# Soft-MoE behind biased attention on one core: last tokens in other buffers, output layers as ordered steps, a new order

## Chip, cores and metric

The kernel runs on one core of one Trainium2 chip. The metric is device microseconds (us) for one execution; the kernel before takes 542.05 us (median of 3 runs, 541.92 to 543.41).

## What is computed

All numbers are float32. First an attention with 8 batches, 8 heads, 576 tokens and 64 numbers a head, with a bias from a small network of the distance between tokens:

```python
scores = scale * np.matmul(q, k.transpose(0, 1, 3, 2))
x = (psi_rel / psi_i)[..., None]
h = np.maximum(x @ w1 + b1, 0.0)
bias = h @ w2
scores = scores + bias.transpose(2, 0, 1)[None, :, :, :]
attn = exp(scores - max) / (sum + 1e-09)
return np.matmul(attn, v)
```

Then a soft mixture of experts over the 4608 tokens of 512 numbers, with 8 experts of 4 slots and hidden size 1024:

```python
logits = x @ phi
slot_input = softmax(logits, axis=0).T @ x
h = np.maximum(slot_input[e] @ w1[e], 0.0)
slot_out[e] = h @ w2[e]
return softmax(logits, axis=1) @ slot_out
```

The softmax over tokens (axis 0) runs over all batches, so the expert layers can begin only when the last batch has been through the attention.

## The kernel before

**Units.** The work is cut into 32 units, one for a pair of heads (hp = 0 to 3) and a batch (b = 0 to 7); unit u is hp * 8 + b. A unit has five (even u) or four blocks p of 128 query rows. A block goes through two score steps S{p}.0 and S{p}.1 on TensorE (PE; 320 and 256 key columns, both heads in each; with a "+" as four 64x64 tiles, line 431, else as two tiles of 64x128, line 425), four steps t{p}.{head}{pass} on VectorE (DVE, line 451) that take the scores out of PSUM, add the bias and keep the running minimum (pass 1 of a head starts from the minimum of pass 0), two exponents e on ScalarE (ACT, line 462), sums m on DVE (469, 470), two scalings n on GpSimd (POOL, 357), transposes T and R on PE (406), copies c and cR out of PSUM (360), and then the product with the values M0, M1, Mr (549), copied out by x0 and x1 to tile xts. The units of hp 0 to 2 write xts to the tensor xs in HBM.

**Tokens.** The units 24 to 31 (hp = 3) fetch the other three head pairs of their batch back from xs: step fx, line 575, tile xo of one buffer, 864 KB. From it come the transposed tokens (K01, K23, KR, copies kc, krc), the logits (L, line 624, copy lc), their repetition over the slots (D), maxima and exponents (d1, d2, d3), the turned weights (W, wc; C, then cA, cB, cC for the softmax over slots) and the sum over tokens (Z, zc). Unit 30 also joins the state of the first seven batches (J1 to J8, F1 to F3).

**Expert layers.** turn_slots() turns the collected slots (line 981); first(j), j = 0 to 7, makes 16 products of 512 columns each (line 996, float32 products show as two instructions); hidden(Q) and turn_hidden(Q) apply the ReLU and turn the result; second(k, Q) is the second layer (1044), gather_slots(k) repeats the slots (1055), and put(k, q) and put_rest(k) multiply by the softmax over slots (1074), copy the products out of PSUM (1024 numbers a row for each half z: z = 0 on ACT, 1 on DVE) and write them out (1083, 1090). The stacked slot weights cT and cR come from the steps A0, A1 with copies Ac0, Ac1 (lines 1024, 1027, 1032, 1033).

**Weights.** 64 tiles of 512 KB, in the order in which the layers need them (fetch_w, lines 874 to 882). 23 go to the buffers "w" during the attention, 24 to buffers that the attention gives back at the end (steps wbm, wbr, wy, wqk, wat, wv, wxo, wxt, wxk), and 17 are refetched to "w" buffers that the first layer has read.

**Order.** Every step is listed by name and unit in ORDER; the program issues the steps sorted by that list, and each engine runs its instructions in that order. All DMAs are issued by SyncE (SP), in the same order, so a DMA that waits for a buffer holds back those behind it. What follows the list was plain code:

```python
for _, _, f in sorted(prog, key=lambda x: x[:2]):
    f()
turn_slots()
for j in range(4):
    first(j)
    refetch(*range(4 * j, 4 * j + (4 if j < 3 else 2)))
hidden(0)
```

Of the kernel before, what the change touches and what calls it, by code (L numbers as in the profile page):

```python
# [36 lines left out]
f28.2/-1 f27.3/-1+ f27.2/-1 f27.1/-1 f34.3/-1 D22/-1 E19/-1 f30.2/-1 B29/-1 E29/-1 f30.0/-1+ D18/-1 D16/-1 f30.1/-1 f34.1/-1
B28/-1 E28/-1 B27/-1 E27/-1 f30.3/-1 f34.2/-1+ D23/-1 D21/-1 D17/-1 f34.0/-1 f24.3/-1+ S1.0/0+ t1.00/0 t1.10/0 f31.2/-1 B30/-1
E30/-1 f31.1/-1 f31.0/-1 f31.3/-1 f24.0/-1+ B34/-1 f24.2/-1 f35.3/-1 E34/-1 f24.1/-1+ f35.0/-1 D19/-1 S0.0/0+ B31/-1 f32.2/-1
f32.1/-1 f35.1/-1 D29/-1 f35.2/-1 B24/-1 f32.0/-1+ f32.3/-1+ D33/-1 E31/-1 t0.10/0 D28/-1 D27/-1 B32/-1 E32/-1+ E24/-1 B35/-1  # L40
S0.1/0 S1.1/0+ E35/-1 S2.0/0 D30/-1 t0.00/0 t0.01/0 t0.11/0 e0.0/0 t1.11/0 e1.1/0 e0.1/0 b2/-1 t1.01/0 e1.0/0 t2.10/0 S2.1/0+
t2.11/0 S3.0/0 D34/-1 e2.1/0 t2.00/0 m0/0 t2.01/0 S0.0/1 D31/-1 D24/-1 D32/-1 n0.1/0 S0.1/1+ e2.0/0 t0.00/1 D35/-1 t0.10/1 t0.01/1
e0.0/1 n0.0/0 S3.1/0 t0.11/1 m1/0 e0.1/1 m2/0 b3/-1 t3.00/0 t3.01/0 t3.10/0 T0/0 c0/0 S4.0/0 n1.1/0 n1.0/0 m0/1 R1/0 n2.1/0 n0.0/1
e3.0/0 t3.11/0 e3.1/0 T1/0 cR1/0+ S4.1/0 S1.0/1 n0.1/1 b4/-1 t4.00/0 t4.10/0 c1/0 S2.0/1 t4.01/0 m3/0 e4.0/0 t4.11/0 t1.10/1
e4.1/0 n2.0/0 t1.00/1 n3.1/0 T2/0 t2.10/1 c2/0 m4/0 S1.1/1 t1.11/1 t2.00/1 n3.0/0 T3/0 t1.01/1 S2.1/1 T0/1 n4.1/0 n4.0/0 c3/0
t2.11/1 t2.01/1 R3/0 cR3/0+ T4/0 w1/8 e1.0/1 R4/0 cR4/0+ c4/0 e2.1/1 S3.0/1+ t3.00/1 t3.10/1 e2.0/1 m2/1 S3.1/1+ e1.1/1 t3.11/1
e3.1/1 m1/1 n2.1/1 lq/2 t3.01/1 e3.0/1 n1.0/1 M0/0 lq/3 M1/0 Mr/0 c0/1 n2.0/1 m3/1 x1/0 x0/0+ S0.0/2+ t0.00/2 t0.10/2 n1.1/1 T1/1
R1/1 cR1/1+ n3.0/1 c1/1 S0.1/2 t0.11/2 t0.01/2 T2/1 c2/1 S1.0/2 n3.1/1 R3/1 cR3/1 t1.10/2 T3/1 c3/1 e0.1/2 t1.00/2 S1.1/2+ t1.01/2
t1.11/2 S3.0/2+ t3.00/2 t3.10/2 lv/2 S2.0/2+ t2.10/2 e0.0/2 m0/2 n0.1/2 t2.00/2 S3.1/2+ t3.01/2 e1.0/2 t3.11/2 e1.1/2 w0/8 M0/1
S2.1/2+ S4.0/2 M1/1 m1/2 e3.0/2 t2.11/2 n0.0/2 t2.01/2 t4.10/2 e3.1/2 m3/2 e2.1/2 e2.0/2 t4.00/2 S4.1/2 t4.11/2 e4.1/2 m2/2 n1.1/2  # L50
n1.0/2 Mr/1 t4.01/2 x0/1 n3.0/2 n3.1/2 T3/2 e4.0/2 lv/3 x1/1+ R1/2 cR1/2 c3/2+ T0/2 c0/2 m4/2 S1.0/3 n2.1/2 t1.10/3 T1/2 n2.0/2
t1.00/3 c1/2 S1.1/3 n4.0/2 t1.11/3 T2/2 t1.01/3 c2/2 n4.1/2 e1.1/3 S0.0/3 S2.0/3 R3/2 t0.00/3 w1/10 t0.10/3 cR3/2+ T4/2 R4/2 cR4/2
t2.10/3 c4/2 t2.00/3 xs/1 S0.1/3+ e1.0/3 t0.01/3 t0.11/3 S3.0/3+ e0.1/3 e0.0/3 S2.1/3+ S3.1/3+ t2.11/3 e2.1/3 m1/3 t2.01/3 e2.0/3
xs/0 t3.10/3 n1.0/3 t3.00/3 M0/2 M1/2 n1.1/3 t3.11/3 m0/3 n0.1/3 t3.01/3 Mr/2 e3.0/3 m2/3 e3.1/3 x0/2 n0.0/3 R1/3 x1/2 cR1/3+ T0/3
m3/3 n2.1/3 n2.0/3 c0/3 lq/4 S1.0/4 T1/3 S1.1/4 t1.00/4 T2/3 t1.10/4 t1.11/4 c1/3 n3.0/3 t1.01/4 c2/3 S2.0/4 t2.10/4 t2.00/4
n3.1/3 T3/3 R3/3 cR3/3+ S0.0/4+ c3/3 e1.0/4 lq/5 S2.1/4+ lv/4 t0.10/4 e1.1/4 t0.00/4 S0.1/4+ t0.11/4 t0.01/4 m1/4 t2.11/4 e0.1/4
t2.01/4 S3.0/4+ t3.00/4 n1.0/4 t3.10/4 M0/3 e0.0/4 m0/4 n1.1/4 S4.0/4 S3.1/4+ t3.01/4 e2.1/4 e2.0/4 xs/2 e3.0/4 t3.11/4 m2/4
e3.1/4 M1/3 S4.1/4 t4.10/4 t4.11/4 e4.1/4 n0.1/4 Mr/3 t4.00/4 t4.01/4 x1/3 n2.1/4 m3/4 x0/3+ e4.0/4 n2.0/4 S1.0/5+ n0.0/4 R1/4
lv/5 cR1/4 t1.00/5 t1.10/5 T0/4 c0/4 S1.1/5 m4/4 t1.01/5 T1/4 n3.0/4 n3.1/4 c1/4 T2/4 t1.11/5 c2/4+ T3/4 c3/4 S0.0/5 n4.1/4 n4.0/4
T4/4 t0.00/5 R3/4 cR3/4 t0.10/5 S2.0/5 R4/4 cR4/4+ S3.0/5+ S0.1/5+ c4/4 M0/4 t2.10/5 t2.00/5 t3.10/5 S2.1/5+ t0.01/5 e1.0/5  # L60
# [155 lines left out]
def body(ctx, tc, qk, v, phi, mw1, mw2, tabh, consth, *outs):  # L216
# [349 lines left out]
    def moe(u):  # L566
# [615 lines left out]
```

## Time and profile before

| | |
|---|---|
| runs | 543.41, 542.05, 541.92 us |
| profiled execution: span, first to last instruction | 539.2 us (the profile gives no other time of it) |
| PE, weight loads, DVE, ACT, POOL busy | 519.7, 351.3, 430.4, 458.4, 223.2 us |
| moved by DMA | 110.18 MB, mean 204 GB/s |
| chain that ended last | PE 75%, DMA 8%, DVE 6%, ACT 5%, issue 3% |

Busy time of an engine is the union of its instructions. The chain goes back from the last instruction to what released it, step by step; "issue" in it is time in which an engine waited for nothing that the profile shows. A DMA's share is that of the core's 16 DMA engines.

### The profile page before, as it was taken

How to read it: one execution, taken by the hardware profiler on the slowest of the kernel's cores; microseconds unless marked ns; L12 is line 12 of the kernel's file. 1: busy time of each engine (PE TensorE's matmuls, PEld its weight loads, DVE VectorE, ACT ScalarE, POOL GpSimd, SP SyncE). 2: the span in 40 equal slices, each digit the busy share in tenths (PEclk: the TensorE clock that was granted, in tenths of full speed). 3: DMA queues.
4: the chain of work that ended last, by engine and by line, in shares of the span. 5: the costliest groups of instructions: out<-in, count | busy, mean ns of one | idle time of the engine just before them, and what ended most of it. 6: DMA issues, size and time to landing. Idle time of an engine off the chain costs nothing.

```text
span 539.2 us, 23170 instructions
## 1 busy us (share of the span) xinstructions
PE 519.7 (96%) x9283; PEld 351.3 (65%) x9283; DVE 430.4 (80%) x1803; ACT 458.4 (85%) x988; POOL 223.2 (41%) x317
## 2 busy tenths in 40 slices
PE   8999899999999999999999999999999999989893
PEld 6444566767767667786776677767777767653661
DVE  6998878889889888989888897988999979661243
ACT  7998999999999999999999999999898889641132
POOL 5200655555455556545456555555233252200000
PEclk9999999999999999999999999999999999999998
DMA  6699536163864435586173658526631446998998
GB/s 216 242 316 348 169 108 195 53 208 113 284 190 150 159 119 173 194 271 168 68 214 111 212 178 273 143 108 199 224 114 43 155 157 242 344 343 329 367 352 321
DMA packets 40795, 110.18 MB, mean 204 GB/s; under 512 B 5360, under 2 KB 5488, under 8 KB 40688
## 3 DMA queue, kind: packets, MB, share of 16 engines
q1 hardware_dynamic: 40688, 108.70, 58.8%
q8 instruction: 73, 1.20, 0.9%
q14 instruction: 34, 0.28, 0.2%
HBM read 81.28 MB, written 27.41 MB: 202 GB/s over the span
## 4 chain that ended last, share of the span: by engine, by line
PE 75%; DMA 8%; DVE 6%; ACT 5%; issue 3%; POOL 1%; SPq 1%; DVEq 0%; ACTq 0%; POOLq 0%
PE ps L549 22%; PE ps L406 16%; PE ps L431 13%; PE ps L425 10%; PE ps L996 3%; PE ps L1044 3%; DMA bias_m<-e 3%; PE ps L1074 2%; DVE y L451 2%; ACT y L462 2%; PE ps L916 2%; DVE f L903 2%; DMA v<-in_v_dram 2%; DMA xo<-xs 1%; PE ps L624 1%
## 5 line engine op out<-in xcount | busy, mean ns | idle before, releaser
L357 POOL TENSOR_SCALAR y<-y,rc 128x576 f32<-128x576 f32 x288 | 211.1, 751 | 218.7 <-DVE rc L470 167.7
L462 ACT ACTIVATE y<-y,mn 128x576 f32<-128x576 f32 x288 | 220.6, 773 | 6.7 <-DVE mn L451 5.5
L549 PE MATMUL ps<-at,v 64*64 64x288 f32 x2304 | 152.2, 403 | 0.5 <-DMA v<-in_v_dram 0.5
L360 ACT COPY at<-ps 128x1024 f32<-128x1024 f32 (+3 forms) x197 | 140.8, 759 | 9.9 <-PE ps L406 7.6
L451 DVE CUSTOM_DVE_ANT_0 y<-ps,bm 128x320 f32<-128x320 f32 x256 | 115.3, 486 | 10.8 <-PE ps L425 4.1
L549 PEld LDWEIGHTS ps<-at,v 64*64 64x64 f32 x2304 | 89.7, 133 | 47.6 <-ACT at L360 1.2
L406 PEld LDWEIGHTS ps<-ident,y 64*128 64x128 f32 x2592 | 98.8, 138 | 33.2 <-POOL y L357 12.4
L451 DVE CUSTOM_DVE_ANT_0 y<-ps,bm,mn 128x256 f32<-128x256 f32 x256 | 113.9, 478 | 6.3 <-PE ps L425 1.1
L406 PE MATMUL ps<-ident,y 64*128 64x64 f32 x2592 | 106.8, 224 | 1.8 <-DVE mn L451 1.0
L431 PE MATMUL ps<-qk 64*64 64x256 f32 (+1 forms) x1280 | 92.9, 407 | 0.1
L425 PE MATMUL ps<-qk 64*128 64x320 f32 (+1 forms) x512 | 86.5, 431 | 1.5 <-DVE mn L451 1.5
L431 PEld LDWEIGHTS ps<-qk 64*64 64x64 f32 x1280 | 45.2, 132 | 28.7 <-ACT at L360 7.0
L462 ACT ACTIVATION_READ_ACCUMULATOR y<-y,mn 128x1 f32 x288 | 56.1, 195 | 0.0
L451 DVE DVE_READ_ACCUMULATOR2_ANT mn<- 128x1 f32 x576 | 47.9, 83 | 0.0
L425 PEld LDWEIGHTS ps<-qk 64*128 64x128 f32 x512 | 42.5, 189 | 7.2 <-DVE mn L451 2.9
L903 DVE TENSOR_SCALAR f<-tabw,offs 128x512 f32<-128x512 f32 (+17 forms) x107 | 40.1, 451 | 1.5 <-DMA bias_m<-e 1.2
L360 DVE COPY at<-ps 128x256 f32<-128x256 f32 (+3 forms) x59 | 34.5, 595 | 7.5 <-PE ps L406 6.4
L916 PE MATMUL ps<-f,wbd 128*32 128x512 f32 (+48 forms) x640 | 39.3, 390 | 0.7 <-ACT e L929 0.5
L916 PEld LDWEIGHTS ps<-f,wbd 128*32 128x32 f32 x640 | 18.2, 110 | 22.4 <-issue 10.5
L469 DVE TENSOR_REDUCE rc<-sm 128x2 f32<-128x4 f32 x144 | 21.9, 152 | 9.9 <-ACT y L462 9.7
L929 ACT ACTIVATE e<-ps,cons 128x591 f32<-128x591 f32 x35 | 26.7, 820 | 2.2 <-PE ps L916 1.9
L470 DVE RECIPROCAL rc<-rc 128x2 f32<-128x2 f32 x144 | 23.9, 166 | 5.0
(142 smaller groups left out, 407.9 us busy)
## 6 DMA issues: line engine op xcount, KB each, us to landing
wt<-in_moe_w_dram SPq DMA_DIRECT2D x62, 512.0 KB, 6.3
qk<-in_qk_dram SPq DMA_DIRECT2D x32, 576.0 KB, 4.3
bias_m<-e SPq DMA_DIRECT2D x32, 295.5 KB, 3.9
v<-in_v_dram SPq DMA_DIRECT2D x32, 288.0 KB, 3.2
bm<-bias_m SPq DMA_DIRECT2D x32, 288.0 KB, 4.8
out_dram<-ob SPq DMA_DIRECT2D x16, 512.0 KB, 3.8
xs<-xts SPq DMA_DIRECT2D x24, 288.0 KB, 4.6
xo<-xs SPq DMA_DIRECT2D x8, 864.0 KB, 5.0
```

What stands on the lines that cost most here:

```text
L357: nc.gpsimd.tensor_scalar(out=out, in0=y, scalar1=r, scalar2=1.0, op0=ALU.mult, op1=ALU.mult)
L360: (nc.vector.tensor_copy if eng else nc.scalar.copy)(out=out, in_=in_)
L406: nc.tensor.matmul(out, src[rs], ident[rs, rs], is_transpose=True, start=True, stop=True, tile_position=(64 * r, 0))
L425: nc.tensor.matmul(pss[hh].t[:, 0:nk], x[rs, S + p * P:S + (p + 1) * P], x[rs, ks], start=True, stop=True, tile_position=(64 * hh, 0))
L431: nc.tensor.matmul(pss[hh].t[64 * r:64 * r + 64, 0:nk], x[rs, q0:q0 + 64], x[rs, ks], start=True, stop=True, tile_position=(64 * hh, 64 * r))
L451: nc.vector.tensor_tensor_reduce(out=heads(hh)[:, cuts[n] // 64:cuts[n + 1] // 64], in0=d["ps", p, n][hh].read()[:, 0:nk].rearrange("a (k ...
L462: nc.scalar.activation(out=y, in_=y, func=AF.Exp, bias=d["mn", p][:, 2 + hh:3 + hh], scale=-1.0, accum_out=d["sm", p][:, hh, 0:1])
L470: nc.vector.reciprocal(out=r, in_=r)
L549: nc.tensor.matmul(d["po"][c].t[o:o + 64, 0:HALF], d["v"][rs, 64 * k:64 * k + 64], at[rs, c, 320 * k + start[c]:320 * k + start[c] + HALF] ...
L903: nc.vector.tensor_scalar(out=f, in0=tabw[:, 0:n], scalar1=off, scalar2=0.0, op0=ALU.add, op1=ALU.max)
L916: nc.tensor.matmul(x[32 * t:32 * t + 32, a:a + c1 - c0], wbd, y, start=True, stop=True, tile_position=(0, 32 * t))
L929: nc.scalar.activation(out=out, in_=x, func=AF.Copy, scale=invs[:, i:i + 1])
```

## The change

**Tokens of the last batch.** Unit 31 no longer uses xo. Its head pairs 0 and 1 go to a buffer of the tag "bm" (step fx, 576 KB), head pair 2 to one of the tag "v" (a new step fy, 288 KB); X(g) reads them there. The refetch step wv, whose buffer is now read until the tokens are turned, may not stand ahead of K23, KR and L.

**Output layers.** The functions behind the list become steps of "unit" 32: the turn of the slots (us, ut, uc, up, uo), j0 to j7 for first(j), h, u and hc for the hidden layer, s for the second layer's quarters, so, g, gc, p, o, O, pr, or, OR for the output, and q0 to q16 for the 17 refetches. Each step issues what the code issued; buffers of the output are looked up by key and no longer handed out in call order, and the engine of a copy (ACT, or DVE with "+") is now the list's choice.

**List.** ORDER is written anew, 2906 entries for 2781. Beside the 125 new entries all names are the same, in another order; 145 score steps have a "+" where 128 had. It is described as a layout that keeps the two score passes of a head apart.

```diff
         def fetch(_):
-            m["xo"] = xp.tile([P, NP - 1, S], F32, name="xo", tag="xo")
-            nc.sync.dma_start(out=m["xo"], in_=xs[b].rearrange("g p j -> p g j"))
+            if fin:
+                x = bsp.tile([P, 2 * S], F32, name="xl", tag="bm")
+                m["xg"] = [x[:, 0:S], x[:, S:2 * S]]
+                nc.sync.dma_start(out=x.rearrange("p (g j) -> p g j", g=2), in_=xs[b, 0:2].rearrange("g p j -> p g j"))
+                return
+            x = xp.tile([P, NP - 1, S], F32, name="xo", tag="xo")
+            m["xg"] = [x[:, g] for g in range(NP - 1)]
+            nc.sync.dma_start(out=x, in_=xs[b].rearrange("g p j -> p g j"))
 
         step(u, "fx", fetch)
+        if fin:
+
+            def fetch_last(_):
+                x = ldp.tile([P, S], F32, name="xl", tag="v")
+                m["xl"] = x
+                nc.sync.dma_start(out=x, in_=xs[b, 2])
+
+            step(u, "fy", fetch_last)
 
         def X(g):
-            return m["xo"][:, g, :] if g < NP - 1 else st[u]["xt"]
+            return st[u]["xt"] if g == NP - 1 else m["xl"] if (u, g) == (31, 2) else m["xg"][g]
 
...
-        step(U - 1, k + {"wv": " Mr", "wxt": " K23 KR L x1"}.get(k, ""), lambda _, home=home: fetch_w(home, several.get(home[1], 1)))
+        step(U - 1, k + {"wv": " Mr K23 KR L", "wxt": " K23 KR L x1"}.get(k, ""), lambda _, home=home: fetch_w(home, several.get(home[1], 1)))
 
...
+    Z = U
...
+        step(Z, "us", scales)
+        step(Z, "ut", turn)
+        step(Z, "uc", keep)
+        step(Z, "up", pick)
+        step(Z, "uo", owner)
...
+        step(Z, f"j{j}", products)
...
+        step(Z, f"h{Q}.0", half0)
+        step(Z, f"h{Q}.1", half1)
+        step(Z, f"u{Q}", turn)
         for z in range(2):
...
+            step(Z, f"hc{Q}.{z}", lambda eng, z=z: keep(eng, z))
...
+        step(Z, f"s{k}{Q}{fq}", products)
...
+        step(Z, f"so{k}", keep_products)
+        step(Z, f"g{k}", gather)
+        step(Z, f"gc{k}", keep)
...
+        step(Z, f"p{k}{q}", products)
         for z in range(2):
...
+            step(Z, f"o{k}{q}{z}", lambda eng, z=z: keep(eng, z))
+            step(Z, f"O{k}{q}{z}", lambda _, z=z: nc.sync.dma_start(out=outs[0][k, q, z], in_=place_out((k, q, z))))
...
+        step(Z, f"pr{k}", products)
         for z in range(2):
...
+            step(Z, f"or{k}{z}", lambda eng, z=z: keep(eng, z))
+        step(Z, f"OR{k}", lambda _: nc.sync.dma_start(out=outs[1][k], in_=place_out(k)))
...
+    for i in range(64 - 47):
+        step(Z, f"q{i}", lambda _, i=i: fetch_w(homeof[i]))
...
     with tc.manual_schedule():
         for _, _, f in sorted(prog, key=lambda x: x[:2]):
             f()
-        turn_slots()
-        for j in range(4):
-            first(j)
-            refetch(*range(4 * j, 4 * j + (4 if j < 3 else 2)))
-        hidden(0)
-        first(4)
-        refetch(*range(16, 19))
-        first(5)
-        turn_hidden(0)
-        first(6)
-        first(7)
-        hidden(1)
```

Three places in the order, as the two programs issue it. First SP, from the last fetches into xo on (xl is the new tile of unit 31's tokens, v the values, wt a weight tile). Before:

```order
L874 DMA wt<-in_moe_w_dram 128x1024 x3
L575 DMA xo<-xs 128x3x576
L874 DMA wt<-in_moe_w_dram 128x1024 x4
L882 DMA wt<-in_moe_w_dram 128x1024 x3
L575 DMA xo<-xs 128x3x576
L882 DMA wt<-in_moe_w_dram 128x1024 x2
```

After:

```order
L913 DMA wt<-in_moe_w_dram 128x1024 x5
L606 DMA xo<-xs 128x3x576
L913 DMA wt<-in_moe_w_dram 128x1024
L358 DMA v<-in_v_dram 128x576
L614 DMA xl<-xs 128x576
L913 DMA wt<-in_moe_w_dram 128x1024
L602 DMA xl<-xs 128x2x576
L913 DMA wt<-in_moe_w_dram 128x1024
L921 DMA wt<-in_moe_w_dram 128x1024 x9
```

Before, the last xo comes behind seven weight loads that follow the one of unit 30; in the changed program the values of unit 31 and its tokens come soon behind the xo of unit 30, with ten weight loads directly behind them.

Next SP's last weight loads and first outputs. Before:

```order
L880 DMA wt<-in_moe_w_dram 128x512 x2
L882 DMA wt<-in_moe_w_dram 128x1024 x5
L880 DMA wt<-in_moe_w_dram 128x512 x2
L882 DMA wt<-in_moe_w_dram 128x1024 x20
L1083 DMA out_dram<-ob 128x1024 x4
```

After:

```order
L919 DMA wt<-in_moe_w_dram 128x512 x2
L921 DMA wt<-in_moe_w_dram 128x1024 x10
L919 DMA wt<-in_moe_w_dram 128x512 x2
L921 DMA wt<-in_moe_w_dram 128x1024 x11
L1174 DMA out_dram<-ob 128x1024 x6
```

Before, the x20 are one load to xo, two to xk and the 17 refetches. After, the x10 are two to xk, one to xo, then the refetches q15 and q4, one to bm, and four more refetches; behind them stand the load to xt (x2) and eleven refetches. So 17 tiles follow from the first refetch on before, and 19 after, and the outputs go out in another grouping.

Last PE, from the end of unit 31 to the first expert layer (L776 or L815 is Z, L826 or L865 F2, L1024 and L1027 or L1096 and L1099 the stacking A, L758 C, L981 or L1030 the turn of the slots, L996 or L1051 the first layer). Before:

```order
L826 MATMUL ps<-acc,rsum 32x128 x4
L1024 MATMUL ps<-ident,ck 32x128 x16
L1027 MATMUL ps<-ident,ck 32x128 x4
L776 MATMUL ps<-xk,ek 32x128 x20
L1024 MATMUL ps<-ident,ck 32x128 x16
L1027 MATMUL ps<-ident,ck 32x128 x4
L981 MATMUL ps<-ident,accs 128x128
L996 MATMUL ps<-wt,sT 32x512 x48
```

After:

```order
L1096 MATMUL ps<-ident,ck 32x128 x16
L1099 MATMUL ps<-ident,ck 32x128 x4
L865 MATMUL ps<-acc,rsum 32x128 x4
L815 MATMUL ps<-xk,ek 32x128 x20
L758 MATMUL ps<-ident,lp 128x32 x5
L1030 MATMUL ps<-ident,accs 128x128
L859 MATMUL ps<-stS_114,rsum 32x1 x4
L1051 MATMUL ps<-wt,sT 32x512 x64
L431 MATMUL ps<-ident,hS 128x64 x32
L1116 MATMUL ps<-wt,hT 32x128 x64
L1096 MATMUL ps<-ident,ck 32x128 x16
L1099 MATMUL ps<-ident,ck 32x128 x4
```

The second stacking (16 + 4 matmuls) stood between Z and the turn of the slots; now it stands behind 64 matmuls of the second layer, C (L758) stands between Z and the turn, and both turns of the hidden layer (x32) stand behind the whole first layer.

## Rows read from the trace of the kernel before

**Rows 1.** The page: span; then busy time, share of the span and instructions.
```profile
span 539.2 us, 23170 instructions
...
PE 519.7 (96%) x9283; PEld 351.3 (65%) x9283; DVE 430.4 (80%) x1803; ACT 458.4 (85%) x988; POOL 223.2 (41%) x317
```

**Rows 2.** Windows, 80 to 440 us: length, busy us per engine, PE clock, DMA share, GB/s.
```profile
80.00:440.00 360.00, 359.07 (x6506) 254.86 (x6500) 314.32 (x1422) 342.82 (x764) 189.12 (x263) 1.00 0.51 165
```

**Rows 3.** Windows, five stretches of the end.
```profile
440.81:469.65 28.84, 27.57 (x590) 19.81 (x586) 23.47 (x90) 23.24 (x55) 7.68 (x12) 1.00 0.74 268
469.65:482.90 13.25, 11.14 (x262) 8.48 (x262) 7.99 (x28) 6.59 (x16) 0.00 (x0) 1.00 1.00 362
483.30:486.80 3.50, 3.50 (x24) 0.89 (x20) 0.10 (x1) 0.00 (x0) 0.00 (x0) 0.51 0.31 122
486.80:499.10 12.30, 12.30 (x128) 3.95 (x124) 1.44 (x2) 1.78 (x3) 0.00 (x0) 1.00 0.97 371
531.50:539.20 7.70, 0.16 (x4) 0.00 (x0) 1.56 (x2) 0.37 (x1) 0.00 (x0) 0.70 0.81 319
```

**Rows 4.** The chain that ended last: start us, us, what.
```profile
461.63 7.98 DMA xo<-xs
...
477.36 0.87 PE ps L1024 x32
478.23 0.22 PE ps L1027 x8
...
479.54 0.64 PE ps L1024 x20
480.18 1.25 issue
481.44 0.52 PE ps L1024 x10
...
482.07 0.22 PE ps L1027 x6
...
482.90 12.20 PE ps L996 x96
495.74 3.57 PE ps L996 x32
```

**Rows 5.** Timeline of SP's queue: start us, us, what it issued.
```profile
437.15 0.33 SPq L333 DMA_DIRECT2D v<-in_v_dram  x1
...
461.63 0.38 SPq L575 DMA_DIRECT2D xo<-xs  x1
```

**Rows 6.** Tile xo: its eight fetches.
```profile
DMA to landing us min/median/max: 4.6/5.0/8.0
```

**Rows 7.** Timeline of PE: start us, us, group, idle before.
```profile
464.00 4.60 PE L549 MATMUL ps<-at,v 64*64 64x288 f32 x72
...
469.65 0.44 PE L624 MATMUL ps<-xo,phis 128*32 128x288 f32 x3 [0.33 <-DMA xo<-xs]
```

**Rows 8.** The chain, in the middle: quartered and whole score steps.
```profile
197.75 0.97 PE ps L431 x16
...
216.64 1.13 PE ps L425 x8
```

**Rows 9.** Timeline of DVE: two passes of one head, one behind the other.
```profile
56.42 0.49 DVE L451 CUSTOM_DVE_ANT_0 y<-ps,bm 128x320 f32<-128x320 f32 x1 [0.56 <-DMA bm<-bias_m]
...
57.07 0.48 DVE L451 CUSTOM_DVE_ANT_0 y<-ps,bm,mn 128x256 f32<-128x256 f32 x1
```

**Rows 10.** Waits of the SP queue from 470 us: total, times, longest us.
```profile
SPq L1083 <- ACT ob L360: 14.5, 7, 7.4
...
SPq L882 <- PE ps L996: 6.7, 4, 5.7
```

**Rows 11.** The page, part 6: count, KB each, us to landing.
```profile
wt<-in_moe_w_dram SPq DMA_DIRECT2D x62, 512.0 KB, 6.3
```

**Rows 12.** Tile v: its fetches.
```profile
DMA to landing us min/median/max: 2.6/3.2/8.5
```

More of the change, by code (lines that the diff above doesn't have):

```diff
@@ L989, in first, with turn, keep @@
+        def turn(_):
+            h = ends["s"] = Banks(1)
+            nc.tensor.transpose(out=h.t[:, 0:P], in_=accs, identity=ident)
+        def keep(eng):
+            sT = ends["sT"] = xp.tile([P, 4, 32], F32, name="sT", tag="ek", bufs=2)
+            cp(eng, sT, ends["s"].read()[:, 0:P].rearrange("a (c s) -> a c s", c=4))
+        step(Z, "us", scales)
[3 more added lines that the diff above has]
+        step(Z, "uo", owner)
     def first(j):
         Q, kc = j // 4, j % 4
-        if kc == 0:
-            ends["h", Q] = Banks(2, 2)
@@ new lines, in first, with hidden_of, half0, half1 @@
+        step(Z, f"j{j}", products)
+    def hidden_of(Q):
+        if ("hS", Q) not in ends:
+            ends["hS", Q] = wp.tile([P, 2, 512], F32, name="hS", tag="w")
+        return ends["hS", Q]
+    def hidden(Q):
+        def half0(_):
+            nc.scalar.activation(out=hidden_of(Q)[:, 0], in_=ends["h", Q].read()[:, 0], func=AF.Relu, scale=ends["own"][:, Q:Q + 1])
+        def half1(_):
+            nc.vector.tensor_scalar(out=hidden_of(Q)[:, 1], in0=ends["h", Q].read()[:, 1], scalar1=ends["own"][:, Q:Q + 1],
+                                    scalar2=0.0, op0=ALU.mult, op1=ALU.max)
+        def turn(_):
+            hT2[Q] = wp.tile([P, 8, P], F32, name="hT", tag="w")
+            h = ends["hp", Q] = Banks(2, 2)
+            for z in range(2):
+                for x in range(4):
+                    for r in range(2):
+                        half_turn(h.t[:, r, 256 * z + 64 * x:256 * z + 64 * x + 64], ends["hS", Q][:, z, x * P:(x + 1) * P], r)
+        def keep(eng, z):
+            cp(eng, hT2[Q][:, 4 * z:4 * z + 4, :].rearrange("a x (r n) -> a r x n", r=2),
+               ends["hp", Q].read()[:, :, 256 * z:256 * z + 256].rearrange("a r (x n) -> a r x n", x=4))
+        step(Z, f"h{Q}.0", half0)
+        step(Z, f"h{Q}.1", half1)
+        step(Z, f"u{Q}", turn)
+        for z in range(2):
+            step(Z, f"hc{Q}.{z}", lambda eng, z=z: keep(eng, z))
@@ L1033, in stacked, with second, products @@
         nc.scalar.copy(out=ends["cR"][:, q], in_=h[:, 1, 0:64])
-    def second(k, Q, parts=(0, 1)):
-        if k == Q == 0:
-            ends["o"] = Banks(2, 99)
-            ends["so"] = wp.tile([P, 2, DM], F32, name="so", tag="w")
-        po = ends["o"].t[:, k % 2, P * (k // 2):P * (k // 2) + P]
-        for fq in parts:
+    def second(k, Q, fq):
+        def products(_):
+            if "o" not in ends:
+                ends["o"] = Banks(2, 99)
+                ends["so"] = wp.tile([P, 2, DM], F32, name="so", tag="w")
+            po = ends["o"].t[:, k % 2, P * (k // 2):P * (k // 2) + P]
             for x in range(4):
@@ L1099, in body @@
         step(U - 1, f"Ac{q}", lambda _, q=q: stacked(q))
+    turn_slots()
+    for j in range(8):
+        first(j)
+    for i in range(64 - 47):
+        step(Z, f"q{i}", lambda _, i=i: fetch_w(homeof[i]))
+    for Q in range(2):
+        hidden(Q)
+    for k in range(4):
+        for Q in range(2):
+            for fq in range(2):
+                second(k, Q, fq)
+        gather_slots(k)
+        for q in range(2):
+            put(k, q)
+        put_rest(k)
     with tc.manual_schedule():
```

458 lines of the change are left out of this document (235 added, 223 removed).

## The prediction

> **What bounds the kernel now.** I read the page first: TensorE (PE) is busy 96% of the span [rows 1]. A mean over stages decides nothing, so next the busy time by stretch. From 80 to 440 us PE is busy 359.07 of 360 us at full clock, VectorE (DVE) 87%, ScalarE (ACT) 95%, the DMA engines half [rows 2]. In that stage nothing is worth anything but PE time itself. Behind 440 us it changes: from 469.65 to 482.90 us PE is busy 11.14 of 13.25 us and the DMA share is 1.00 at 362 GB/s; then come 3.5 us at half the clock with the DMA share at 0.31, then 0.97 again [rows 3]. So the end has two owners, PE's chain and the bytes still to be moved, and I sum it for both. The chain of waits then shows where the end loses time: 7.98 us of "DMA xo<-xs", 1.25 us of "issue", 12.20 us for the first 96 matmuls of the first expert layer [rows 4].
>
> The durations come from the profiled execution, whose span is 539.2 us [rows 1]. The median of the runs is 542.05 us; the 2.85 us outside the span I carry over unchanged. A difference below 0.3% (1.6 us) I take as no change.
>
> **The tokens of the last batch.** Before, the fetch for unit 31 needs tile xo, which unit 30 still reads, so SP issues it only at 461.63 us, between weight loads [rows 5]; it lands 8.0 us later, against a median of 5.0 [rows 6]. The chain shows all 7.98 us, but PE is not idle in them: the 72 matmuls of the last attention product run until 468.6, and PE idles 0.33 us before the logits [rows 7]. The logits need the two evictions that follow that product as well. So the fetch is worth 0.3 us, not 8, as long as the product stands where it stands. After the change the two-thirds part waits for a bias buffer that DVE frees and the third for a v buffer, both about 10 us of PE work ahead of use.
>
> **Before the first expert layer.** L/31 to the first layer takes 13.25 us. In the new PE order the second stacking (A1) no longer stands ahead of the turn of accs, but behind the first half of the second layer. That takes its 1.4 us of matmuls (0.64, 0.52 and 0.22) and the 1.25 us "issue" wait inside it out of this stretch [rows 4]. The wait has no releaser in the profile, so nothing ties it to A1; I count it as gone here, and its return elsewhere stands under rival 2. The rest of the serial chain (logits, D, exponent, W, Z, the turn of accs) is unchanged, its short waits too. Sum: 0.3 + 1.4 + 1.25 = 3.0 us earlier.
>
> **The new list in the middle.** 145 score steps run as quarters instead of 128 (of 256 that have the choice). Two quartered steps cost 0.97 us, two whole ones 1.13 [rows 8], up to 0.08 us for one; 17 of them give 1.4 us at most, and nothing if only the widths behind the two rows differ. I take 0.5. The places on PE where one tile shape follows another number 117 in the old list and 116 in the new by my count: nothing. Eight copies, net, go from ACT to DVE; both work beside PE and neither ends its waits in the middle: nothing, and DVE as the cover (87%) is not gone with 8 us more at 1 us a copy, 89%. Bounds for the rest of the list, which cannot be read step by step: PE's gaps from 80 to 440 us are under 1 us together [rows 2], so no more can be won there; a late load could cost 2 us. I take 0. Sum: 0.5 us; the first layer starts at 482.9 - 3.5 = 479.4.
>
> The two passes of a head "kept apart": I count in the DVE sequence of the lists 21 heads whose second pass directly follows the first before, and 32 after. So the list does not do this. A direct follower starts 0.65 us after a predecessor that lasts 0.49 [rows 9], so 0.16 us of DVE stand idle; 11 more of them make 1.8 us, hidden behind PE in the middle, and 1.8 on the path where DVE is late.
>
> **From the first layer on, by PE.** Before: 482.9 to 531.5, 48.6 us, and 7.7 us from there to the end [rows 3]. A1 comes back with the pace of A0, 0.87 + 0.22 = 1.1 us [rows 4]. Of the first layer, 96 matmuls took 12.20 us where three times the next 32 (3.57) make 10.7: 1.5 us went to the stretch at a granted clock of 0.51, the lower level, after a stretch with PE idle for a sixth [rows 3, 4]. With that stretch shorter I count half of it back, 0.75. Whatever stands in the list as a step instead of a call changes nothing by itself: each step issues the same matmuls and copies. The order of products, evictions and outputs differs by a few rows at the end only; I count 0. End by PE: 479.4 + 48.6 + 1.1 - 0.75 + 7.7 = 536.0.
>
> **By DMA.** The first refetch of a weight tile takes the oldest of the 23 w buffers and waits until the first layer's first products are done; SP waited 5.7 us for that [rows 10], the share fell to 0.31 and came back by 486.8 [rows 3]. From 486.0, as I take it inside that dip, 17 tiles of 512 KB [rows 11] (0.524 MB) and the outputs, 4608 x 512 numbers or 9.44 MB, are moved: 18.35 MB in 53.2 us, 345 GB/s. In the new SP order two more tiles stand behind that wait, one in a bm buffer that the token fetch now holds, one in xt: 19 tiles, 19.4 MB. At 345 GB/s that is 56.2 us, at the 371 of the best stretch [rows 3] 52.3; I take the middle, 54.2, since weights and outputs now follow each other without SP's wait of 7.4 us for the first output copy [rows 10]. The refetch starts 3.5 us earlier plus some 0.3 for the clock, 482.2. End by DMA: 482.2 + 54.2 = 536.4, 534.5 to 538.4.
>
> The stretches show 362 and 371 GB/s with the share at 0.97 to 1.00, and I hold that for the limit of this kernel's mix. [...]
>
> The later of the two, with 0.2 us for their collisions, gives a span of 536.6 and **539.4 us**, 2.6 less than 542.05.
>
> **Rivals.**
> 1. *PE sets the end and the list closes more gaps* (faster). From 440.81 to 469.65 us PE has 1.27 us of gaps [rows 3], the first 80 us have others; if the list closes 1.5 us of these and the rest of the half clock goes (0.75), PE's end is 533.8 and the time 536.6, if the DMA engines keep up. Against it: the share of 1.00. [...]
> 2. *The gain at the first layer goes elsewhere* (no change). The values of unit 31 were issued at 437.15, 27 us ahead of their product at 464.0 [rows 5, 7]; now SP issues them behind six weight loads and the tokens of unit 30, by my count of PE work about 9 us ahead. v lands in 3.2 us (median) to 8.5 [rows 12]. With a full queue PE can wait 1 to 2 us there, and "issue" waits recur: the first layer starts 2 us later than summed, the end is 538.6 and the time 541.4.
> 3. *The bytes decide, and they come later* (slower). If the first layer starts no earlier than before and the bytes move at the old 345 GB/s, the two tiles behind SP's wait cost 1.05 MB or 3.0 us in full: 486.0 + 56.2 = 542.2, a time of 545.0. It is slower by more than 0.3% once the refetch starts after 484.6, the first layer after some 481.5. For it: the DMA share. Against: A1 is gone from that stretch whatever else happens.
> 4. *The two passes are not apart, and DVE is late*: 539.4 + 1.8 = 541.2, no change. Against: DVE is idle 13% of the middle [rows 2].
>
> **How the numbers follow.** Forecast 0.40 (its own range 537.4 to 541.4, the two rates of the bytes), rival 1 0.20, rival 2 0.22, rival 3 0.14, rival 4 0.04. Faster: 0.36 of the forecast and rival 1 make 0.56. No change: the remaining 0.04, 0.18 of rival 2 and rival 4 make 0.27, with a little of rival 3. Slower: the rest, 0.17. The range runs from 535.0 (most of rival 1) to 543.9 (rival 3 half paid).
>
> **What would show it.** Right: no wait for the tokens of unit 31; the first layer's first matmul at 478.5 to 480.5 us; PE still busy over 99% from 80 to 440; DMA share at 0.95 or more from some 482 us to the last outputs; last weight issue near 502. Wrong: a first layer at 482 or later, PE waiting for v of unit 31 or for bm ahead of it, a dip of the DMA share longer than 3.5 us, or an end that follows the last matmul by 7 us as before with DMA idle between (then PE owns it).

## The result and the profile after

The changed kernel takes 546.69 us (median of 14 runs, 544.90 to 550.17), the kernel before 541.98 us beside it (14 runs, 540.41 to 546.33). The ratio is 1.0081, 95% interval [1.0058, 1.0105]: some 4.4 us slower. I had forecast 539.4 us, range 535.0 to 543.9. It is not the forecast, and the median lies above the range.

The profiled execution of the changed kernel took 544.9 us with a span of 542.8 us, and is the quickest of its 14 runs; single places below are therefore read from it, and sizes are taken from the ratios of many runs. From its page, against [rows 1]: span and busy times, the queue that carries instructions (packets, MB, share), and the shares of the chain.

```profile
span 542.8 us, 23306 instructions
...
PE 520.3 (96%) x9351; PEld 358.0 (66%) x9351; DVE 432.2 (80%) x1815; ACT 456.0 (84%) x976; POOL 222.5 (41%) x317
...
q8 instruction: 73, 1.20, 0.9%
...
PE 86%; DVE 4%; DMA 3%; ACT 3%; issue 2%; POOL 1%; SPq 0%; DVEq 0%; POOLq 0%; ACTq 0%
```

The stretches of the changed kernel, columns as in [rows 2]; they answer to [rows 2, 3].

```profile
52.00:60.00 8.00, 6.49 (x68) 3.58 (x64) 6.45 (x34) 7.27 (x17) 4.39 (x6) 0.79 0.76 236
...
80.00:440.00 360.00, 359.19 (x6540) 260.70 (x6536) 311.14 (x1419) 341.52 (x755) 186.35 (x259) 1.00 0.50 161
...
473.37:484.27 10.90, 9.77 (x238) 7.30 (x237) 6.61 (x19) 5.78 (x13) 0.00 (x0) 1.00 0.85 297
484.27:497.60 13.33, 13.33 (x124) 4.06 (x128) 6.44 (x26) 1.64 (x6) 0.00 (x0) 1.00 0.94 362
497.60:528.30 30.70, 27.16 (x678) 19.36 (x672) 11.11 (x16) 9.09 (x15) 0.00 (x0) 1.00 0.95 372
528.30:535.70 7.40, 5.09 (x52) 2.27 (x42) 3.66 (x5) 3.25 (x6) 0.00 (x0) 0.91 1.02 404
```

The middle is what it was: PE is busy 359.19 of 360 us, and from the first attention product to that of unit 30 it takes 385.1 us (454.11 less 68.99), before 385.2 (452.00 less 66.81). The stretch from L of unit 31 to the first layer fell from 13.25 to 10.9 us, and the 128 matmuls of the first layer from 15.8 us [rows 4] to 14.0 (the window of 13.33 us holds 124 of them), at full clock. So what I forecast as a gain is there, some 4 us of it, and the kernel is slower all the same. Three places show where the time went. First PE's timeline in the changed kernel: the first attention product, L of unit 30, the product of unit 31, L of unit 31 (idle before a group in brackets).

```profile
68.99 4.60 PE L574 MATMUL ps<-at,v 64*64 64x288 f32 x72
...
462.11 0.44 PE L663 MATMUL ps<-xo,phis 128*32 128x288 f32 x3 [1.35 <-DMA xo<-xs]
...
468.79 3.63 PE L574 MATMUL ps<-at,v 64*64 64x288 f32 x56 [0.32 <-issue]
...
473.30 0.44 PE L663 MATMUL ps<-xl,phis 128*32 128x288 f32 x3
```

The first product starts at 68.99 us where before it started at 66.81: 2.2 us are lost in the start, of which 52 to 60 us show a granted clock of 0.79 (before 1.00). And the wait for tokens is not gone; it went from unit 31 (no bracket now; 0.33 in [rows 7]) to unit 30. The SP queue says why:

```profile
437.24 16.45 SPq L913 DMA_DIRECT2D wt<-in_moe_w_dram  x5
453.79 0.38 SPq L606 DMA_DIRECT2D xo<-xs  x1
...
457.51 0.43 SPq L358 DMA_DIRECT2D v<-in_v_dram  x1
...
460.81 0.38 SPq L602 DMA_DIRECT2D xl<-xs  x1
```

Five weight loads stand ahead of the tokens of unit 30. The last waits for the bias passes of unit 31 on DVE, so the tokens are issued at 453.79 us and take 8.19 us more. The chain of the changed kernel, at that place, in the first layer and at the end:

```profile
453.32 0.02 DVE mn L476
...
453.36 0.33 SPq L913
...
453.79 8.19 DMA xo<-xs
...
484.27 13.98 PE ps L1051 x128
...
505.09 1.43 issue
...
511.38 1.36 issue
...
531.48 1.24 DVE ob L385
...
533.93 1.24 DVE ob L385
```

In the second layer two "issue" waits of 1.4 us stand on the chain where before one of 1.25 stood ahead of the first layer [rows 4] and one of 0.86 in the second. At the end PE waits twice for output copies on DVE (1.9 us together; before 0.6 us for copies on ACT). From the start of the first matmul of the second layer to the start of the last of all the kernel before takes 32.3 us, the changed one 35.3: 1.1 us of that is the second stack (A1), which stands there now; the 32.3 hold the second turn, which the change has ahead of the layer.

### The profile page after: what moved, and what is told of

Its sections match the earlier page's. It is cut to its first block, busy times and chain, and to the rows that moved or that the text cites. A ratio compares the mean times of both kernels' runs of the same rounds, so it can differ in the third digit from the quotient of the medians.

```text
span 542.8 us, 23306 instructions
## 1 busy us (share of the span) xinstructions
PE 520.3 (96%) x9351; PEld 358.0 (66%) x9351; DVE 432.2 (80%) x1815; ACT 456.0 (84%) x976; POOL 222.5 (41%) x317
## 4 chain that ended last, share of the span: by engine, by line
PE 86%; DVE 4%; DMA 3%; ACT 3%; issue 2%; POOL 1%; SPq 0%; DVEq 0%; POOLq 0%; ACTq 0%
PE ps L574 25%; PE ps L431 18%; PE ps L456 16%; PE ps L450 11%; PE ps L1116 3%; PE ps L1051 3%; PE ps L1159 2%; DMA bias_m<-e 2%; PE ps L955 2%; PE ps L663 2%; DMA xo<-xs 2%; ACT e L968 1%; DVE y L476 1%; DVE f L942 1%; PE ps L278 1%
## 5 line engine op out<-in xcount | busy, mean ns | idle before, releaser
L574 PEld LDWEIGHTS ps<-at,v 64*64 64x64 f32 x2304 | 95.2, 133 | 43.8 <-ACT at L385 1.9
L456 PE MATMUL ps<-qk 64*64 64x256 f32 (+1 forms) x1416 | 104.3, 410 | 0.8 <-DVE mn L476 0.8
L450 PE MATMUL ps<-qk 64*128 64x320 f32 (+1 forms) x444 | 77.4, 434 | 0.5 <-DVE mn L476 0.4
L456 PEld LDWEIGHTS ps<-qk 64*64 64x64 f32 x1416 | 52.5, 133 | 30.0 <-ACT at L385 5.1
L450 PEld LDWEIGHTS ps<-qk 64*128 64x128 f32 x444 | 37.3, 189 | 5.6 <-DVE mn L476 2.3
L385 DVE COPY at<-ps 128x256 f32<-128x256 f32 (+3 forms) x65 | 36.9, 582 | 4.6 <-PE ps L431 3.7
```

Of the source, the lines that this page charges most:

```text
L385: (nc.vector.tensor_copy if eng else nc.scalar.copy)(out=out, in_=in_)
L450: nc.tensor.matmul(pss[hh].t[:, 0:nk], x[rs, S + p * P:S + (p + 1) * P], x[rs, ks], start=True, stop=True, tile_position=(64 * hh, 0))
L456: nc.tensor.matmul(pss[hh].t[64 * r:64 * r + 64, 0:nk], x[rs, q0:q0 + 64], x[rs, ks], start=True, stop=True, tile_position=(64 * hh, 64 * r))
L574: nc.tensor.matmul(d["po"][c].t[o:o + 64, 0:HALF], d["v"][rs, 64 * k:64 * k + 64], at[rs, c, 320 * k + start[c]:320 * k + start[c] + HALF] ...
```

## Experiments

The list can be edited freely, so parts were moved one at a time. t1, t8, t10 and t11 have the list of before, the others the changed one. All ratios are to the kernel before, on the same chip. The rows come from three chips, so two rows are compared by their ratios; the difference of two is uncertain by about 0.003, or 1.6 us.

| run | list | edit | median us | ratio, interval |
|---|---|---|---|---|
| t0 | new | none | 546.68 | 1.0079 [1.0052, 1.0105] |
| t2 | new | tokens of unit 30 ahead | 543.80 | 1.0044 [1.0026, 1.0062] |
| t5 | new | t2 + start of before | 543.24 | 1.0036 [1.0016, 1.0057] |
| t6 | new | t2 + first turn early | 546.70 | 1.0099 [1.0067, 1.0130] |
| t7 | new | t2 + outputs of before | 542.12 | 1.0010 [0.9989, 1.0031] |
| t9 | new | t2 + t5 + t7 | 541.31 | 0.9990 [0.9974, 1.0006] |
| t1 | old | tokens in other buffers | 541.56 | 0.9991 [0.9971, 1.0010] |
| t8 | old | t1 + A1 behind first layer | 540.06 | 0.9972 [0.9953, 0.9992] |
| t10 | old | t8 + new end | 540.82 | 0.9983 [0.9962, 1.0004] |
| t11 | old | t8 + tokens of unit 30 late | 545.47 | 1.0068 [1.0045, 1.0092] |
| t3, t4 | new | first tries of t5, t7 | 548.98, 553.39 | 1.0143 [1.0110, 1.0176], 1.0210 [1.0180, 1.0241] |

**t0, the changed kernel again.**

> The changed kernel itself once more, beside the others on the same chip. Theory: 546.7 us as in its 14 runs, ratio 1.007 to 1.010; its profile shows the same places: about 69 us at the token-wide product of unit 0, a wait for xo at L of unit 30, 7.3 us from the last product of the second layer to the last matmul. Rival: its median depends on the session, and it comes out at 544 to 545, so that the gain of t2 was smaller than it looked.

546.68 us: it does not depend on the session. This time PE's wait ahead of L of unit 30 carries another name (timeline of PE in t0):

```profile
463.29 0.44 PE L663 MATMUL ps<-xo,phis 128*32 128x288 f32 x3 [1.44 <-DVE acc L829]
```

The tokens were issued at 454.88 us and the slowest fetch of that tile took 8.3, to 463.18; the DVE operation ended at 463.24. Of two waits the later is named. t2 tells which one counted: there L starts before that operation of DVE does.

**t1, the buffers alone.** The steps instead of plain code are in it too; with the old order they issue the old instructions.

```diff
-... m3/31 wbm3/31 T1/31 ... fx/31 ... j7/32 ...
+... m3/31 T1/31 ... fx/31 fy/31 ... j7/32 wbm3/31 ...
```

> The list of before and the order of its end, with the token input of the last batch in the other buffers and nothing else changed (one weight load gives up its early place to it and stands behind the first layer). Theory 1, the loss lies in the new list and its places, not in the buffers: the product of unit 31 no longer waits for its tokens (0.3 us), the rest is as before, 541 to 542 us, ratio to before 0.998 to 1.000. Theory 2, the buffers themselves cost, because the load of weights that gave up its place comes late and the first layer waits for it: 543 to 546 us.

541.56 us. No wait for xl is left, and no loss by the later weight load shows; a gain of the 0.3 us I had given to the fetch is too small to be seen. In its chain an issue wait of 1.63 us stands inside A1, the place where before has 1.25 [rows 4]. The half clock does not stand where before has it. Chain of t1, first layer and second:

```profile
484.64 10.51 PE ps L1051 x96
...
509.81 3.31 PE ps L1116 x64
```

The 96 matmuls that took 12.20 us before [rows 4] take 10.51; behind another issue wait, of 1.27 us, 64 matmuls of the second layer take 3.31 us where others take 1.89, at a granted clock of 0.54.

**t2, tokens of unit 30 ahead.**

```diff
-... m0/31 n0.1/31 wbm3/31 n0.0/31 cR3/30+ wbm4/31 M0/30 e1.1/31 S3.1/31+ fx/30 ...
+... m0/31 n0.1/31 fx/30 wbm3/31 n0.0/31 cR3/30+ wbm4/31 M0/30 e1.1/31 S3.1/31+ ...
```

> The changed kernel with one edit: the token fetch of unit 30 stands ahead of the two weight loads on the transfer queue that wait for the last bias pass. Theory 1, the delay of 1.2 us at unit 30 is passed on to the end: 545.3 us where the changed kernel has 546.7, no wait for xo at L of unit 30. Rival, the layers behind are paced by their weights, so that what is gained at unit 30 is lost in waits for weights: 546.7 us, with the product of the first layer starting 1.2 us earlier and ending at the same time.

SP and PE of t2:

```profile
452.09 0.38 SPq L606 DMA_DIRECT2D xo<-xs  x1
...
461.05 0.43 PE L663 MATMUL ps<-xo,phis 128*32 128x288 f32 x3
```

The fetch is issued 2.8 us earlier than in t0 and the bracket is gone. The ratio falls by 0.0035, 1.9 us (the medians say 2.9; the wait in the two profiles was 1.4), little more than its uncertainty. The profiles agree: from the first product to the first layer t2 takes 413.2 us, the changed kernel and t0 415.3 each. Passed on to the end: theory 1.

**t11, the converse: the same delay put into the list of before.**

```diff
-... c3/30 fx/30 e0.1/31 ... m1/31 wbm4/31 n0.0/31 ...
+... c3/30 e0.1/31 ... m1/31 wbm4/31 fx/30 n0.0/31 ...
```

> The kernel of t8 with one fetch moved on the transfer queue: the tokens of unit 30 behind the loads that wait for the last bias pass, as the change has it. Theory 1, the wait at L of unit 30 appears and is passed on: 1.2 to 2.9 us more than 540.06, 541.3 to 543.0 us. Rival, in the list of before the last bias pass comes early enough and nothing waits: 540.1 us.

5.4 us slower than t8, more than I expected. SP and PE of t11:

```profile
441.61 15.28 SPq L913 DMA_DIRECT2D wt<-in_moe_w_dram  x6
457.29 0.38 SPq L606 DMA_DIRECT2D xo<-xs  x1
...
464.84 0.71 PE L431 MATMUL ps<-ident,xo 64*128 64x64 f32 x16 [4.27 <-DMA xo<-xs]
```

The tokens are issued 3.5 us later than in the changed kernel and needed at the same time. PE stands still for 4.3 us, and from 464.6 to 468.0 us the granted clock is 0.64. One entry of a list of 2906 is worth 1%.

**t3 and t5, the start.** The entries of "unit" -1 build the bias; there the two lists part. The first try took before's order up to M0 of unit 2.

```diff
-... E33/-1 B23/-1 E23/-1 B17/-1 E17/-1 f27.3/-1+ B19/-1 E19/-1 f28.1/-1+ ...
+... E33/-1 f28.3/-1 B23/-1 E23/-1 f28.1/-1+ f29.3/-1 B17/-1 E17/-1 f27.0/-1 B19/-1 ...
```

> The changed kernel with the steps up to the first token-wide product of unit 2 in the order of before, and the new order from there on. Theory 1, the new order of the start costs 2.2 us: first such product of unit 0 at 66.8 us of the profile instead of 69.0, the end 2.2 us earlier, 544.5 us. Rival, the half clock is a cost paid once, at the start (52 to 60 us) in the changed kernel and in the first layer in before: with the start of before it comes back in the first layer, worth 2.5 us there, and the time stays at 546.7 us or a little above.

It measured the seam. The new list fetches the values of units 4 and 3 in that order, the old one 3 before 4; cut there, SP waits for a v buffer with the queries of unit 4 behind it. Chain of t3:

```profile
95.40 0.13 SPq L358
...
95.59 3.85 DMA qk<-in_qk_dram
```

t5 cuts ahead of M0 of unit 1, where both have fetched the same, and stands on t2:

> The kernel of t2 (tokens of unit 30 ahead) with the steps up to the second token-wide product, that of unit 1, in the order of before; the cut lies where both lists have fetched the same heads, so that the transfer queue keeps one order. Theory 1, the new order of the start costs about 2 us for good: that product of unit 1 at 77 us instead of 80, the end at 541.7 to 542.2 us where t2 has 543.8. Rival, the half clock that the new order pays at 52 to 60 us comes back later (in before it stood in the first layer, 2.5 us there): the product of unit 1 at 77 us all the same, but 543.5 to 544.5 us at the end, with a half clock behind 400 us.

PE of t5: the first product, and that of unit 31.

```profile
67.20 4.59 PE L574 MATMUL ps<-at,v 64*64 64x288 f32 x72
...
464.40 5.34 PE L574 MATMUL ps<-at,v 64*64 64x288 f32 x72
```

t2 starts the first product at 70.01 and that of unit 31 at 466.78, so 2.8 and 2.4 us are won. But the first layer starts only 1.0 us earlier (482.21 against 483.19), the last matmul ends 0.8 us earlier, and the ratio falls by 0.0008, inside its interval. No half clock comes back before the end (1.00 from 52 to 62 and from 80 to 440 us; the mean of the execution is 0.994, in the changed kernel 0.989), so the rival's reason is not it either (nor is it worth 2.5 us: by t1 it cost the first layer 1.7). Where the 1.6 us go is seen: the product of unit 31 takes 5.34 us instead of 4.60, and issue waits sum to 3.7 us behind 440 us where t2 has 2.8. Why they grew stays open.

**t4 and t7, the outputs.** t4 put the products, copies and stores of the output in the order of before, and left weight loads between them.

```diff
-... p00/32 q11/32 o000/32 Ac1/31 s110/32 s111/32 so1/32+ q2/32 p01/32 o010/32 o001/32+ ...
+... p00/32 q11/32 Ac1/31 o000/32 O000/32 o001/32+ O001/32 s110/32 s111/32 q2/32 so1/32+ ...
```

> The changed kernel with the steps from the second product block of the second layer on in the order of before: output products, their copies and the stores, the store of o000 first and the copy o001 ahead of so1. Theory 1, the new order of copies and stores costs the last 1.0 us behind the last product of the second layer and part of the late first store: from the last such product to the last matmul 6.2 us instead of 7.3, 545.2 to 545.7 us. Rival, the end is held by the transfers (share 1.02 at 404 GB/s from 528 to 536 us) whatever the order of copies: 546.7 us.

Waits of SP in t4, 495 to 530 us (total, times, longest), and a piece of its chain:

```profile
SPq L1174 <- ACT ob L385: 12.7, 1, 12.7
```
```profile
518.99 10.27 DMA wt<-in_moe_w_dram
```

SP stood 12.7 us in front of the first store, with weight loads behind it; from 503.4 to 519.0 us the DMA share was 0.54, and then PE waited 5.1 us for those weights. It says nothing of the copies. t7 puts all loads ahead of the first store:

```diff
-... p00/32 q11/32 o000/32 Ac1/31 s110/32 s111/32 so1/32+ q2/32 p01/32 o010/32 o001/32+ ...
+... p00/32 q11/32 q2/32 q3/32 ... q14/32 o000/32 O000/32 o001/32+ Ac1/31 O001/32 s110/32 ...
```

> The kernel of t2 with output products, copies and stores in the order of before, and all weight loads ahead of the first store this time (in t4 weight loads stood behind stores on the transfer queue and were late, which is what that run measured). Theory 1, the changed kernel's order of copies and stores costs the 1.0 us more behind the last product of the second layer: from it to the last matmul 6.2 us, not 7.3, first store at about 512 us of the profile instead of 515, 542.6 to 543.0 us. Rival, the transfers hold the end: 543.8 us.

542.12 us, 0.0034 or 1.8 us under t2. SP's first store in t7:

```profile
509.94 5.49 SPq L1174 DMA_DIRECT2D out_dram<-ob  x4
```

The first store goes out 5.1 us earlier than at 515.04 us in the changed kernel, since o001 no longer stands behind so1 on DVE and the first store is that of the first copy. From the second layer's first matmul to the last matmul it takes 33.4 us (t2: 35.1). Waits of PE for copies behind 495 us, two rows of t2 and one of t7:

```profile
PE ps L1159 <- DVE ob L385: 1.9, 2, 1.3
PE ps L1159 <- ACT so L385: 0.4, 1, 0.4
```
```profile
PE ps L1159 <- ACT ob L385: 0.6, 2, 0.3
```

2.3 us became 0.6, and that is the whole 1.7. The earlier store is not seen to pay: from the end of the last matmul to the end of the span it is 7.0 us in t2 and 7.2 in t7.

**t10, the converse: the new end behind the list of before.** As t8, with all entries from j0 on in the order of the change.

> The kernel of t8 (list of before, tokens in other buffers, second stack behind the first layer; 540.06 us) with the end of the changed kernel from the first layer on: both turns behind the eighth step, its order of output products, copies and stores. Theory 1, the loss of the end goes with its order: 1.7 us as t7 gave back plus up to 0.8 us for the turns, 541.8 to 542.6 us. Rival, the order of outputs costs only where the copies run late behind the new list: 540.0 to 540.5 us.

540.82 us, 0.6 to 0.8 us above t8, which neither proves a loss nor excludes 1.7. The same two waits for DVE are in its chain:

```profile
526.75 1.24 DVE ob L385
...
529.20 1.24 DVE ob L385
```

From the last matmul of the second layer to the last of all it takes 7.1 us in t10 and t2, 6.2 in t8 and t7. So 0.9 us at the very end go with the order. The profiles show the rest too: from the first matmul of the first layer to the last of all it takes 50.4 us in t10 and 48.9 in t8, as it takes 51.4 in t2 and 49.7 in t7. One profile each; the medians and ratios do not confirm that the loss is as large behind the old list.

**t6, the first turn early.** In the change both turns stand behind the first layer, which leaves 2.1 us between the layers, 1.4 of them the turns themselves (before none; the expectation's 2.7 lets the first layer end too early). I took that for a loss.

```diff
-... j3/32 h0.1/32 ... j5/32 ... h0.0/32 ... h1.1/32 u0/32 hc0.1/32+ u1/32 ... hc0.0/32 ...
+... j3/32 h0.1/32 h0.0/32 ... j5/32 u0/32 hc0.0/32 hc0.1/32+ ... h1.1/32 u1/32 ...
```

> The kernel of t2 with the turn of the first half of the hidden rows, and its copies, between the sixth and the seventh step of the first layer as in before. Theory 1, the gap of 2.7 us between the layers comes from both turns standing there and their copy being waited for: the gap falls to 0.4 to 1.2 us and the end moves by the wait alone, 0.8 us, 543.0 us (the turn's own matmuls are needed in either place). Rival, the second layer is held by instruction fetches and transfers: 543.8 us.

2.9 us slower than t2. Chain, then PE's timeline, of t6:

```profile
494.73 0.69 DVE hT L385
...
500.84 0.67 DVE hS L1067
```
```profile
501.55 0.47 PE L431 MATMUL ps<-ident,hS 64*128 64x64 f32 x8 [3.42 <-DVE hS L1067]
```

Between these two DVE works 5.4 us on other things, most of it the softmax over slots for the last batches, which the new list has left for the first layer. The early copy holds that back, it holds back the second half of the hidden rows, and PE waits 3.4 us. The gap belongs to this list and pays.

**t8, A1 alone.**

```diff
-... wxt/31 wxo/31 A1/31 Ac0/31 wxk/31 Ac1/31
+... wxt/31 wxo/31 Ac0/31 wxk/31 ... s011/32 A1/31 ... o001/32+ Ac1/31 ...
```

> The kernel of t1 (list of before, tokens in other buffers) with the second stack of token weights moved behind the first layer, to where the change has it. The prediction's term alone: 2.6 us leave the stretch ahead of the first layer, 1.1 come back behind it: 541.56 - 1.5 = 540.0 us, ratio to before 0.996 to 0.998, no issue wait of 1.25 to 1.8 us ahead of the first layer. Rival, the issue wait goes where the stack goes (in the changed kernel it stood inside it at 505 us) and the first layer is held by its weights: 541.5 us.

540.06 us, below both kernels: 0.9972 [0.9953, 0.9992]. Under t1 it is 1.5 us by the medians and 1.0 by the ratios, which is not clear of noise. Windows of t8, from L of unit 31 to the first layer, and the first layer:

```profile
470.20:481.17 10.97, 9.65 (x234) 7.21 (x226) 7.77 (x30) 6.56 (x16) 0.00 (x0) 1.00 0.93 324
481.17:495.70 14.53, 14.53 (x144) 4.65 (x148) 1.82 (x5) 1.80 (x3) 0.00 (x0) 1.00 1.01 379
```

13.25 us [rows 3] became 10.97, with no issue wait in it; the only larger one behind 440 us is 1.0 us in the second layer. From L of unit 31 to the last matmul t1 takes 62.7 us and t8 59.9. Of these 2.8 us, 1.4 are the half clock in t1's second layer, which t8 does not have; 1.4 are left for the block.

**t9, three repairs together.** As t7, with the start of t5.

> The changed kernel with three places put back: tokens of unit 30 ahead (t2), start up to the product of unit 1 in the order of before (t5), outputs in the order of before (t7). Theory 1, the three add up: 543.8 - 0.6 - 1.7 = 541.5 us, no slower than before, which would leave the rest of the new list worth nothing either way. Rival, what one saves the other loses, since the end is paced by transfers and instruction fetches: 542.1 to 542.5 us.

541.31 us, as theory 1 has it: t0 minus t9 is 0.0089, 4.8 us, where the single steps gave 1.9, 0.4 and 1.8. The loss of the change is in these three places together; that the start has a part in it is not clear of noise (t5), and for the last 0.7 us the intervals are too wide. Waits of PE in t9 behind 495 us:

```profile
PE ps L1116 <- issue: 3.2, 2, 1.7
PE ps L1116 <- ACT hT L385: 0.8, 1, 0.8
PE ps L1159 <- ACT ob L385: 0.6, 2, 0.3
```

t8 is lower still, 1.2 us by the medians and 1.0 by the ratios, which is inside the noise. The issue waits are 2.2 us fewer there; that they make the difference was not tried.

## Why the prediction was wrong

In the profile of the changed kernel the first layer starts at 484.27 us, forecast 479.4: 2.2 us were lost ahead of the first product, 1.4 in the wait at unit 30. From there to the last matmul it takes 51.3 us, forecast 49.0. My first sign of being wrong, a first layer at 482 or later, came. By the prediction's own steps:

- *"The order of products, evictions and outputs differs by a few rows at the end only; I count 0."* This is one of two failed steps: 1.8 us (t7, where the whole order of the end was put back). Few rows, but on the last copies PE waits with nothing else to do, 2.3 us in t2 and 0.6 in t7.
- *"Bounds for the rest of the list ... a late load could cost 2 us. I take 0."* The other: the tokens of unit 30, 1.9 us (t2). I named them once, as something that v of unit 31 stands behind, and never asked what they stand behind themselves. The order rows of SP showed five loads ahead of them. v of unit 31, which I did watch, made nobody wait.
- *The first 80 us* had no term. The trace lost 2.2 us there; at the end t5 gave back 0.4 us, which is not clear of noise.
- *A1 and its issue wait, -1.4 and -1.25, and 1.1 back.* Borne out by the stretch, 13.25 us to 10.97 in t8. The sum of 1.55 has 1.5 in the medians beside it and 1.0 in the ratios, so its size is not settled. In the changed kernel the wait came back, as 1.43 and 1.36 us in the second layer: that clause of rival 2 held.
- *Half of the half clock, 0.75.* The whole of it left the first layer, 1.7 to 1.8 us and not 1.5, and 52 to 60 us got a stretch of it (a granted clock of 0.79). That the shorter stretch ahead freed the layer is not shown: t1 keeps A1 and a longer wait there (1.63 us for 1.25), and has the layer's 96 matmuls in 10.51 us all the same, the pace that the changed kernel has at a clock of 1.00 (13.98 for 128).
- *The tokens of unit 31, 0.3.* Not contradicted (t1), too small to see. *The quarters, 0.5:* the middle gained 0.1 us in all (385.2 to 385.1).
- *Steps alone cost nothing.* Right (t1). *The passes kept apart:* the list does not do it, and it cost nothing in the middle.
- *"362 and 371 GB/s ... the limit of this kernel's mix."* Wrong: 404 GB/s at a share of 1.02 in the changed kernel, 379 at 1.01 in t8. The bytes did not set the end, PE did: it has 86% of the chain, and no transfer stands in that between the first layer and the last copy.

Rival 3 named the nearest time, 545.0. Its condition came true, a first layer no earlier than before, but its mechanism did not happen: SP waited at most 1.6 us for a w buffer that the first layer reads, not 5.7, and the bytes moved at 362 to 404 GB/s up to the last matmuls, not 345. That its time came close is luck.

## What to carry to other kernels

Where one queue issues all transfers, list for every late fetch what stands ahead of it and when the last of these can be issued: one entry moved here cost 2 us in one list and 5 in another. A new order is not one change: cost its start, the last fetches and the last copies one by one, and where a list allows it measure them so, at places where both orders have done the same. A forecast gain can be there and the whole be slower: with the list of before, the other buffers and the one moved block the kernel is 0.3% faster than before (t8), though how much of that is the block's is not clear of noise. A number that fits a sum proves little while a stretch of low clock can fall into one profile and not into the other: 0.51 in the first layer before, where 96 matmuls take 12.20 us, and 10.51 us for them in t1.

## What the hardware showed

**PE's issue waits.** Issue waits of 0.4 to 1.7 us recur behind 470 us, wherever the list puts the work. DMA in the changed kernel from 504.0 to 506.5 us, around the first of them (queue: packets, MB, share):

```profile
q1 hardware_dynamic: 272, 1.00, 100.4%
q8 instruction: 1, 0.02, 2.7%
```

One packet of queue 8 lies in this stretch, and one just ahead of the wait at 511.38 us, both with the transfers at 100%. The queue moves 73 packets in 1.20 MB, 16.4 KB each, in the changed kernel and in the one before. That a wait of this kind is PE standing for instructions that are not there yet is my reading: the profile names no releaser, and does not say which engine a packet serves. A1's wait stands behind the same 20 of its 40 matmul records in t1 (1.63 us) as before (1.25), and behind 38 of them in the changed kernel (1.43), where other code stands ahead of it.

In the middle, with a share of 0.50, PE is idle for 0.81 us in all, though 52 of the 73 packets fall there. From that I take full queues for the reason of the waits, and t4, where SP sent nothing for a while, had them in part only. Its chain, then the window behind its first wait:

```profile
508.26 1.15 issue
...
512.82 1.88 PE ps L1116 x64
```
```profile
509.40:513.50 4.10, 4.09 (x110) 3.14 (x113) 0.59 (x1) 1.03 (x3) 0.00 (x0) 1.00 0.01 4
```

Its first wait stands where the changed kernel has it, with the share at 1.04 from 506 to 507 us, when the packet of queue 8 starts, and at nothing during the wait. The second is gone: its packet falls in the window above, and the 64 matmuls in which the changed kernel waits run through at the same pace. One run and one wait; the reason is argued, not shown.

**The half clock follows the start of the list.** One profile of each program shows it. In the stretch from 52 to 62 us, five of the six programs with the new start show a granted clock of 0.83 to 0.85 (t6 shows 1.00), and all eight with the start of before 1.00. 0.79 over the 8 us from 52 to 60 makes 3.4 us at the 0.50 that the windows 57 to 58 and 58 to 59 us show in the changed kernel; PE had been idle for 0.40 us two us ahead of it and stood idle for 1.11 us where it began. The late start is not the clock's alone: the six programs with the new start begin the first product at 69.0 to 70.8 us, t6 without the low clock at 69.06, the eight with the start of before at 66.7 to 68.2. Its cost at the end is not more than what t5 gave back.
